# Routing without two-SBUF-input vector steps, one whole-row load of A, shared transpose banks, and first loads planned with the rest, in a fused linear-attention and mixture-of-adapters kernel

## The chip, the cores and the metric

The kernel runs on one core of one Trainium2 chip. The metric is the device time of one execution in microseconds (us), as the median over several executions. One profiled execution of each kernel gives a trace; its span is about 1.8 us shorter than the time of the same execution (span 137.4 us for 139.16 us in the kernel before), so spans and times are not mixed below.

Five engines matter. PE is the matrix engine (PEld is its weight load), DVE the vector engine, ACT the scalar engine, POOL the GpSimd engine, and SP only issues DMA transfers. Each works through its own list of instructions in order: in the trace of the kernel before, ACT stands 16.97 us at one step whose input has not come, and does none of its later steps meanwhile. SBUF is the on-chip memory that the loads fill. PSUM is the memory that PE writes its results to, here in banks that the steps take and give back.

On this one core a run is called slow when it is more than 1.5% above the fastest run of the same kernel in its call. Slow does not mean a lower clock here: in the first call the slow runs of the kernel before had granted PE clocks of 0.942 to 0.971, the fast ones 0.936 to 0.973.

## The reference

Linear attention with cosine and sine weights of the position, then a top-2 mixture of rank-16 adapters on its result. Sizes: 8 batches, 8 heads, 576 positions, 64 per head, so x has 4608 rows of 512.

```python
# attention, per batch and head
r = np.maximum(x, 0.0)
phi(x) = np.concatenate([r * cos_w, r * sin_w], axis=-1)        # 64 -> 128
kv  = einsum('bhsf,bhsd->bhfd', phi(k), v);   z = sum_s phi(k)
num = einsum('bhsf,bhfd->bhsd', phi(q), kv);  den = phi(q) . z + 1e-06
x   = (num / den), heads side by side: 4608 x 512
# adapters
logits = x @ w_gate                     # 8 experts
w, e   = softmax over the two largest logits
out    = x + sum over those two of w * ((x @ A[e]) @ B[e])      # A: 512x16, B: 16x512
```

## The kernel before

The program is a list of named steps, each with an engine, a modelled cost, a priority, the steps it depends on and the buffers it takes and gives back. A planner written in Python simulates them when the kernel is built and emits them in its simulated order. On the chip that order is fixed: if the model is wrong about when something is ready, the engine simply waits there.

```python
def plan(ops, bufs, slack=0.12):
    ...        # per engine: earliest possible start s of each candidate
        for e, c in by_eng.items():
            s0 = min(c)[0]
            pick = min((x for x in c if x[0] <= s0 + slack), key=lambda x: (x[1], x[0]))
            if best is None or pick[0] < best[0]:
                best = pick
    ...
```

The steps of one batch: SP loads k, q and v (1.18 MB each); ACT makes kp = phi(k), in 9 pieces of two instructions; POOL casts v to bf16 (vb); PE accumulates kvz from kp and vb, and ACT copies it to kvs. The steps of one group g of 128 rows (36 groups; two half-groups of 64 rows each): POOL scales q (qp), PE transposes it (qTp), DVE copies it out with the relu (qT), PE multiplies with kvs (nd), DVE normalises (rden, then xt), PE transposes (xTp), DVE copies (xT), PE makes logits and x·A together (za). Every third group the routing follows for three groups at once: DVE (m8, lm, u, ge), ACT (sigmoid sg), DVE (wg, zg), PE and DVE (zTp, zT), then PE makes dx, ACT copies it (osb) and SP stores it. Each pair of batches has nine groups: four of the first batch, four of the second, and a last one shared by both. So both q buffers of a pair come free only when POOL has done the qp of the shared group. There are three buffers each for k, q and v.

The parts that the change touches:

```python
    # loads of batch 0 first, written out ahead of the plan; then A, in four
    # scattered loads (runs of 16 floats, 64 bytes)
    for name in "kqv":
        for a in range(2):
            load(name, 0, a, 2)
    ...
    for ci in range(DCH):
        nc.sync.dma_start(out=AWf[:, ci, 0:ER],
                          in_=moe_A[:, ci * 128:(ci + 1) * 128, :].transpose([1, 0, 2]))
    ...
    # routing
    nc.vector.tensor_tensor(out=lm, in0=m8[:, :, 0], in1=m8[:, :, 1], op=ALU.add)
    ...
    ge = p_sm.tile([NP, TRI, E], FP32, name="ge")              # in SBUF
    nc.vector.tensor_tensor(out=ge, in0=lg, in1=m8[:, :, 1:2].to_broadcast(...), op=ALU.is_ge)
    ...
    nc.vector.tensor_tensor(out=wg, in0=ge, in1=sg, op=ALU.mult)
    ...
    # the plan: loads of batch 0 depend on "start" and emit nothing;
    # loads of later batches depend on their buffer alone
    op("start", "none", 0.0, 0, none, lat=2.2)
    op("weights", "none", 0.0, 0, none, lat=15.0)
    ...
    # the qp of one half-group; the shared group gives both q buffers back
    op(("qp", g, y), "POOL", 0.91, p - 14 + 4 * y, ...,
       give=["qf"] if b in done else [])
```

PSUM banks: `big` 2 (kvz, nd), one for qTp, one shared by xTp and zTp, one for za, one for dx.

Of the kernel before, what the change touches and what calls it, by code (L numbers as in the profile page):

```python
# [12 lines left out]
ALU = mybir.AluOpType  # L13
# [12 lines left out]

def plan(ops, bufs, slack=0.12):

# [6 lines left out]
    for n, o in ops.items():  # L35
# [3 lines left out]
        if not o.deps:  # L39
            cand.append(n)  # L40
    order = []
    while waiting:
        best = None
        by_eng = {}
        for n in cand:
            o = ops[n]
            if any(not free[p] for p in o.take):
                continue
            s = max([eng_free.get(o.eng, 0.0)]
                    + [ops[d].end + (ops[d].lat if ops[d].eng != o.eng else 0.0) for d in o.deps]  # L50
                    + [min(free[p]) for p in o.take])
            by_eng.setdefault(o.eng, []).append((s, o.prio, n))
        for e, c in by_eng.items():
            s0 = min(c)[0]
            pick = min((x for x in c if x[0] <= s0 + slack), key=lambda x: (x[1], x[0]))
            if best is None or pick[0] < best[0]:
                best = pick
        if best is None:
            raise RuntimeError(f"no step can go: {sorted(waiting)[:20]}")
        s, _, n = best  # L60
        o = ops[n]
        o.start, o.end = s, s + o.cost
        eng_free[o.eng] = o.end
        for p in o.take:
            free[p].remove(min(free[p]))
        for p in o.give:
            free[p].append(o.end + o.lat)
        cand.remove(n)
        del waiting[n]
        for m in succ.get(n, ()):  # L70
            nblock[m] -= 1
            if nblock[m] == 0:
                cand.append(m)
        order.append(n)
# [4 lines left out]
def kernel(  # L79
# [43 lines left out]
    ps_big = ctx.enter_context(tc.tile_pool(name="ps_big", bufs=2, space=PS))  # L123
    ps_qt = ctx.enter_context(tc.tile_pool(name="ps_qt", bufs=1, space=PS))
    ps_tp = ctx.enter_context(tc.tile_pool(name="ps_tp", bufs=1, space=PS))
    ps_za = ctx.enter_context(tc.tile_pool(name="ps_za", bufs=1, space=PS))
# [5 lines left out]
    def load(name, b, a, parts):  # L132
        src = {"q": q, "k": k, "v": v}[name]
        if a == 0:
# [5 lines left out]
            in_=dv[:, a * n:(a + 1) * n])  # L140

    for name in "kqv":
        for a in range(2):
            load(name, 0, a, 2)

# [25 lines left out]

    AWf = persist.tile([NP, DCH, ER + E], FP32, name="AWf")
    for ci in range(DCH):
        nc.sync.dma_start(  # L174
            out=AWf[:, ci, 0:ER],
            in_=moe_A[:, ci * 128:(ci + 1) * 128, :].transpose([1, 0, 2]),
        )
    nc.sync.dma_start(
        out=AWf[:, :, ER:ER + E],
        in_=moe_w_gate.rearrange("(c p) e -> p c e", p=128),  # L180
    )
    Bf = persist.tile([NP, DM], FP32, name="Bf")
    nc.sync.dma_start(out=Bf, in_=moe_B.rearrange("e r d -> (e r) d"))
    AW = persist.tile([NP, DCH, ER + E], BF16, name="AW")
    Ball = persist.tile([NP, DM], BF16, name="Ball")

    def weights_cast(i):
        nc.vector.tensor_copy(*((AW, AWf), (Ball, Bf))[i])

# [53 lines left out]
    st = [dict() for _ in range(G)]  # L243
    tri_za, tri_zgT = {}, {}

# [9 lines left out]
    def q_t(g):  # L255
        qps = st[g].pop("qp")
        qTp = ps_qt.tile([NP, HP, 2, 2, SP], BF16, name="qTp")
        for y, qp in enumerate(qps):
# [40 lines left out]
    def x_t(g):  # L299
        xt = st[g]["xt"]  # L300
        xTp = ps_tp.tile([NP, DCH, NP], BF16, name="xTp", tag="tp")
        for c in range(DCH):
# [10 lines left out]
    def za_mm(g):  # L313
        t, i = divmod(g, TRI)
        xT = st[g].pop("xT")
        if i == 0:
            tri_za[t] = ps_za.tile([NP, TRI, ER + E], FP32, name="za")
        za = tri_za[t]
# [6 lines left out]
    def route_a(t):  # L325
# [3 lines left out]
        for i in range(TRI):  # L329
            nc.vector.max(out=m8[:, i, :], in_=za[:, i, ER:ER + E])  # L330

        lm = p_sm.tile([NP, TRI], FP32, name="lm")
        nc.vector.tensor_tensor(out=lm, in0=m8[:, :, 0], in1=m8[:, :, 1], op=ALU.add)  # L333
        u = p_sm.tile([NP, TRI, E], FP32, name="u")
        nc.vector.scalar_tensor_tensor(out=u, in0=lg, scalar=2.0,
                                       in1=lm.to_broadcast([NP, TRI, E]),
                                       op0=ALU.mult, op1=ALU.subtract)
        ge = p_sm.tile([NP, TRI, E], FP32, name="ge")
        nc.vector.tensor_tensor(out=ge, in0=lg,
# [23 lines left out]
    def z_t(t):  # L363
        zg = tri_zgT[t]
        zTp = ps_tp.tile([NP, TRI, NP], BF16, name="zTp", tag="tp")
        for i in range(TRI):
# [24 lines left out]
    def store(g):  # L391
        osb = st[g].pop("osb")
        for y, (b, x) in enumerate(groups[g]):
# [5 lines left out]
          "kvs": 4, "xt": 8, "xT": 3, "zT": 3, "osb": 12,  # L399
          "big": 2, "qTp": 1, "tp": 1, "za": 1, "dx": 1}  # L400
    ops = {}

    def op(name, *args, **kw):
        ops[name] = Op(*args, **kw)
# [5 lines left out]
    LEAD = 2  # L410
    op("start", "none", 0.0, 0, none, lat=2.2)
    op("weights", "none", 0.0, 0, none, lat=15.0)
    for i in range(2):
        op(("w", i), "DVE", 0.35, 10 + 10 * i, lambda i=i: weights_cast(i), deps=["weights"])
    for b in range(B):
        for n, name in enumerate("kqv"):
            due = 10 * GB * (b - LEAD) + 4 * n
            parts = 2 if b == 0 else 1
            for a in range(parts):
                if b == 0:  # L420
                    op(("ld", name, b, a), "SP", 0.65, due, none, deps=["start"],
                       take=[name + "f"] if a == 0 else [], lat=1.3)
                else:
                    op(("ld", name, b, a), "SP", 0.65, due,
                       lambda name=name, b=b: load(name, b, 0, 1),
                       take=[name + "f"], lat=1.3)
                op((name, b, a), "DMA", 3.02 / parts, due, none,
                   deps=[("ld", name, b, a)], lat=0.4)
# [22 lines left out]
    for g in range(G):  # L451
# [4 lines left out]
        for y in range(2):  # L456
# [5 lines left out]
        op(("qt", g), "PE", 0.45, p - 4, lambda g=g: q_t(g),  # L462
           deps=[("qp", g, 0), ("qp", g, 1)], take=["qTp"], give=["qp"] * 2)
        op(("qr", g), "DVE", 0.6, p - 2, lambda g=g: q_relu(g),
           deps=[("qt", g)], take=["qT"], give=["qTp"])
        op(("nd", g), "PE", 0.35 if len(bs) == 1 else 0.5, p + 2, lambda g=g: attn(g),
# [4 lines left out]
        op(("xT", g), "PE", 0.23, p + 10, lambda g=g: x_t(g),  # L471
           deps=[("xt", g)], take=["tp"])
        op(("xo", g), "DVE", 0.34, p + 12, lambda g=g: x_out(g),
           deps=[("xT", g)], take=["xT"], give=["tp"])
        op(("za", g), "PE", 0.26, p + 16, lambda g=g: za_mm(g),
           deps=[("xo", g), ("w", 0)], take=["za"] if i == 0 else [], give=["xT"])
        if i == TRI - 1:
# [5 lines left out]
            op(("zt", t), "PE", 0.17, p + 21, lambda t=t: z_t(t),  # L483
               deps=[("rb", t)], take=["tp"])
            op(("zo", t), "DVE", 0.3, p + 22, lambda t=t: z_out(t),
               deps=[("zt", t)], take=["zT"], give=["tp"])
        p = 10 * (3 * t + 2) + 24 + 6 * i
        op(("dx", g), "PE", 0.45, p, lambda g=g: dx_mm(g),
           deps=[("zo", t), ("w", 1)], take=["dx"],
           give=["xt"] + (["zT"] if i == TRI - 1 else []))  # L490
# [37 lines left out]
```

## Time and profile before

| | before |
|---|---|
| median time | 140.7 us (139.75 to 141.67, 3 runs) |
| span of the profiled run, granted PE clock | 137.4 us, 0.960 |
| first rden on DVE (the first normalised group) | 31.8 us |
| first to last rden | 92.3 us, of which DVE is busy 84.5 |
| after the last rden's start | 13.4 us |

The page of the kernel before: busy time of each engine; then digits, one for each of 40 slices of the span (3.4 us each), the busy tenths of the slice (row DMA: the core's DMA engines); the DMA rate in the same slices; and the engines' shares of the chain of work that ended last.

```profile
PE 90.7 (66%) x1580; PEld 66.9 (49%) x1580; DVE 95.1 (69%) x268; ACT 81.8 (60%) x193; POOL 84.4 (61%) x170
...
DVE  0263230027999999889869898999989899995500
...
POOL 4009960499599795999980899999599900000000
...
DMA  4999899999999999999999999598932727162765
GB/s 134 366 376 202 160 376 402 393 392 389 391 393 380 394 397 405 389 394 401 373 394 398 395 392 339 149 211 207 372 107 57 177 57 172 24 159 51 182 159 118
...
DVE 47%; PE 23%; SPq 10%; ACT 9%; DMA 5%; issue 3%; ACTq 0%
```

No engine is busy more than 69% of the span, but DVE is at eight or nine tenths (once six) from the eleventh slice until the tail: it bounds the middle. Before that DVE does little, but for the third and the tenth slice, and the DMA rate dips to 202 and 160 GB/s in two of them.

The timeline of the kernel before, lines of SP, ACT, DVE and POOL. The columns are start, duration, engine, source line, operation, output and input, number of instructions, and in brackets the idle time just before and what ended it. For a line of SP (SPq) the duration is the time in which it issued, waits between its issues included.

```profile
3.81 9.45 SPq L174 DMA_DIRECT2D AWf<-in_moe_A_dram  x4
...
14.52 0.43 SPq L138 DMA_DIRECT2D kf<-in_k_dram  x1
...
20.92 0.51 ACT L204 ACTIVATE kp<-kf,cos_tab 128x256 bf16<-128x256 f32 x1 [16.97 <-DMA kf<-in_k_dram]
...
30.50 0.57 ACT L231 CAST kvs<-kvz 128x520 bf16<-128x520 f32 x1
...
31.76 0.21 DVE L290 RECIPROCAL rden<-nd 128x8 f32<-128x8 f32 x1 [1.57 <-PE nd L277]
...
62.18 2.42 DVE L333 TENSOR_TENSOR lm<-m_1306 128x3 f32<-128x3 f32 x1
...
62.18 2.23 POOL L212 CAST vb_130<-vf 128x1152 bf16<-128x1152 f32 x2
...
76.13 0.48 POOL L250 TENSOR_SCALAR qp<-qf,cos_tab 128x256 bf16<-128x256 f32 x1 [4.42 <-DMA qf<-in_q_dram]
```

Three things are to be seen. The four scattered loads of A hold SP for 9.45 us, so k of batch 1 is issued only at 14.52. The planner had placed kp of batch 1 ahead of kp of batch 0 in ACT's list, so ACT waits 16.97 us for that k, and kvs of batch 0, which the first group needs, comes at 30.50. And a DVE step on three columns, lm, took 2.42 us beside two POOL casts.

Durations of the same step over its 12 and 36 executions, from the tile view of the kernel before: minimum, median and maximum in ns, then the first and the last start in us.

```profile
L353 DVE TENSOR_TENSOR wg<-ge,sg x12: 173/294/634, 39.9 to 128.3; 128x24 f32<-128x24 f32 x12
...
L290 DVE RECIPROCAL rden<-nd x36: 197/207/209, 31.8 to 124.0; 128x8 f32<-128x8 f32 x36
```

The stretch from first to last rden, from the windows view of the kernel before: the stretch and its length, busy us (instructions) of PE, PEld, DVE, ACT and POOL, then granted PE clock, DMA share and GB/s.

```profile
31.76:124.03 92.27, 79.34 (x1448) 59.98 (x1446) 84.53 (x236) 64.08 (x155) 67.86 (x133) 0.96 0.86 292
```

### The profile page before, as it was taken

How to read it: one execution, taken by the hardware profiler on the slowest of the kernel's cores; microseconds unless marked ns; L12 is line 12 of the kernel's file. 1: busy time of each engine (PE TensorE's matmuls, PEld its weight loads, DVE VectorE, ACT ScalarE, POOL GpSimd, SP SyncE). 2: the span in 40 equal slices, each digit the busy share in tenths (PEclk: the TensorE clock that was granted, in tenths of full speed). 3: DMA queues.
4: the chain of work that ended last, by engine and by line, in shares of the span. 5: the costliest groups of instructions: out<-in, count | busy, mean ns of one | idle time of the engine just before them, and what ended most of it. 6: DMA issues, size and time to landing. Idle time of an engine off the chain costs nothing.

```text
span 137.4 us, 4094 instructions
## 1 busy us (share of the span) xinstructions
PE 90.7 (66%) x1580; PEld 66.9 (49%) x1580; DVE 95.1 (69%) x268; ACT 81.8 (60%) x193; POOL 84.4 (61%) x170
## 2 busy tenths in 40 slices
PE   0004200459886998993699999878998996967430
PEld 0003100358674865772587668555766865644100
DVE  0263230027999999889869898999989899995500
ACT  7100009999078999985538986993899142321440
POOL 4009960499599795999980899999599900000000
PEclk9999999999999999999559999999999999999995
DMA  4999899999999999999999999598932727162765
GB/s 134 366 376 202 160 376 402 393 392 389 391 393 380 394 397 405 389 394 401 373 394 398 395 392 339 149 211 207 372 107 57 177 57 172 24 159 51 182 159 118
DMA packets 23331, 38.55 MB, mean 281 GB/s; under 512 B 6288, under 2 KB 6288, under 8 KB 23312
## 3 DMA queue, kind: packets, MB, share of 16 engines
q1 hardware_dynamic: 23312, 38.30, 83.9%
q8 instruction: 12, 0.20, 0.6%
q14 instruction: 7, 0.06, 0.1%
HBM read 28.85 MB, written 9.44 MB: 279 GB/s over the span
## 4 chain that ended last, share of the span: by engine, by line
DVE 47%; PE 23%; SPq 10%; ACT 9%; DMA 5%; issue 3%; ACTq 0%
DVE xt L292 15%; SPq L174 7%; ACT kp L204 7%; DVE qT L266 7%; DVE xT L310 6%; DMA kf<-in_k_dram 5%; DVE zg L355 5%; DVE rden L290 4%; PE dx L382 4%; PE kvz L224 4%; DVE lm L333 3%; PE nd L277 3%; PE za L320 3%; PE xTp L303 3%; PE qTp L260 2%
## 5 line engine op out<-in xcount | busy, mean ns | idle before, releaser
L250 POOL TENSOR_SCALAR qp<-qf,cos_tab 128x256 bf16<-128x256 f32 x72 | 34.8, 483 | 20.0 <-DMA qf<-in_q_dram 20.0
L204 ACT ACTIVATE kp<-kf,cos_tab 128x256 bf16<-128x256 f32 x66 | 33.1, 502 | 17.0 <-DMA kf<-in_k_dram 17.0
L250 POOL TENSOR_SCALAR qp<-qf,sin_tab 128x256 bf16<-128x256 f32 x72 | 35.0, 487 | 0.0
L266 DVE TENSOR_SCALAR qT<-qTp 128x1024 bf16<-128x1024 bf16 x36 | 24.6, 682 | 14.7 <-PE qTp L260 14.6
L388 ACT COPY osb<-dx 128x512 f32<-128x512 f32 x36 | 20.9, 580 | 23.0 <-PE dx L382 22.8
L260 PE MATMUL qTp<-ident,qp 128*128 128x128 bf16 x288 | 24.6, 233 | 12.6 <-POOL qp L250 11.8
L204 ACT ACTIVATE kp<-kf,sin_tab 128x256 bf16<-128x256 f32 x66 | 32.8, 497 | 0.0
L292 DVE TENSOR_TENSOR xt<-nd,rden 128x512 bf16<-128x512 f32 x36 | 24.9, 691 | 1.2
L260 PEld LDWEIGHTS <-qp 128*128 128x128 bf16 x288 | 18.9, 104 | 13.9 <-POOL qp L250 12.9
L224 PEld LDWEIGHTS <-kp 64*128 64x128 bf16 x576 | 11.2, 99 | 14.6 <-ACT kp L204 11.6
L303 PE MATMUL xTp<-ident,xt 128*128 128x128 bf16 x144 | 14.8, 228 | 5.2 <-DVE xt L292 5.1
L310 DVE COPY xT<-xTp 128x512 bf16<-128x512 bf16 x36 | 15.1, 419 | 3.4 <-PE xTp L303 2.5
L277 PE MATMUL nd<-kvs,qT 128*128 128x65 bf16 x256 | 14.5, 202 | 3.6 <-DVE qT L266 1.9
L381 PE MATMUL dx<-xt,ident 128*128 128x512 bf16 x36 | 13.9, 386 | 3.9 <-ACT osb L388 3.5
L320 PE MATMUL za<-AW,xT 128*128 128x136 bf16 x144 | 15.0, 229 | 2.1 <-DVE zg L355 1.3
L382 PE MATMUL dx<-Ball,zT 128*128 128x512 bf16 x36 | 14.0, 388 | 2.2 <-DVE zT L373 1.8
L277 PEld LDWEIGHTS <-qT 128*128 128x128 bf16 x256 | 11.4, 104 | 7.3 <-DVE qT L266 4.1
L303 PEld LDWEIGHTS <-xt 128*128 128x128 bf16 x144 | 10.1, 101 | 9.9 <-DVE xt L292 6.6
L320 PEld LDWEIGHTS <-xT 128*128 128x128 bf16 x144 | 10.7, 101 | 5.3 <-issue 1.6
L224 PE MATMUL kvz<-vb_128,kp 64*128 64x65 bf16 x216 | 5.9, 208 | 11.0 <-ACT kp L204 11.0
L290 DVE RECIPROCAL rden<-nd 128x8 f32<-128x8 f32 x36 | 7.3, 204 | 4.2 <-PE nd L277 3.3
L231 ACT CAST kvs<-kvz 128x520 bf16<-128x520 f32 x8 | 4.7, 592 | 8.8 <-PE kvz L224 8.7
(73 smaller groups left out, 84.1 us busy)
## 6 DMA issues: line engine op xcount, KB each, us to landing
out_dram<-osb SPq DMA_DIRECT2D x72, 128.0 KB, 3.0
kf<-in_k_dram SPq DMA_DIRECT2D x7, 1152.0 KB, 10.3
qf<-in_q_dram SPq DMA_DIRECT2D x7, 1152.0 KB, 7.9
vf<-in_v_dram SPq DMA_DIRECT2D x7, 1152.0 KB, 13.1
kf<-in_k_dram SPq DMA_DIRECT2D x2, 576.0 KB, 4.1
qf<-in_q_dram SPq DMA_DIRECT2D x2, 576.0 KB, 7.2
vf<-in_v_dram SPq DMA_DIRECT2D x2, 576.0 KB, 9.2
AWf<-in_moe_A_dram SPq DMA_DIRECT2D x4, 64.0 KB, 7.3
```

What stands on the lines that cost most here:

```text
L204: nc.scalar.activation(kp[:, :, i, :], tin["k", b][:, :, x, :], AF.Relu, bias=0.0, scale=tab[:, x:x + 1])
L224: nc.tensor.matmul(out=kvz_t[b][:, e, i * W:(i + 1) * W], lhsT=kps[b, x][ps, i], rhs=vb[ps, i, x, :], start=(x == 0), stop=(x == X - 1))
L250: nc.gpsimd.tensor_scalar(out=qp[:, :, i, :], in0=tin["q", b][:, :, x, :], scalar1=tab[:, x:x + 1], scalar2=1.0, op0=ALU.mult, op1=ALU.mult)
L260: nc.tensor.transpose(out=qTp[:, i, :, y, :], in_=qp[:, i], identity=ident)
L266: nc.vector.tensor_scalar_max(qT, qTp.rearrange("f i e y p -> f (i e) (y p)"), 0.0)
L277: nc.tensor.matmul(out=nd[:, gg, cs], lhsT=qT[:, h, :], rhs=kv_sb[b0][:, h, :], start=True, stop=True)
L292: nc.vector.tensor_tensor(out=xt, in0=nd_v[:, :, :, 0:D], in1=rden.rearrange("p (g j) -> p g j", g=2).to_broadcast([NP, 2, 4, D]), op=ALU. ...
L303: nc.tensor.transpose(out=xTp[:, c, :], in_=xt[:, c * 128:(c + 1) * 128], identity=ident)
L310: nc.vector.tensor_copy(xT, xTp)
L320: nc.tensor.matmul(out=za[:, i, :], lhsT=xT[:, c, :], rhs=AW[:, c, :], start=(c == 0), stop=(c == DCH - 1))
L382: nc.tensor.matmul(out=dx, lhsT=zT[:, i, :], rhs=Ball, start=False, stop=True)
L388: nc.scalar.copy(osb, dx)
```

## The change

Its intent: take away the routing steps of DVE that read two SBUF operands, because they contend with POOL; take A's scattered loads out of SP's way by loading whole 2 KB rows and turning them with 16 PE transposes; let the three kinds of transposes share two rotating banks; and let the planner know that batch 0's loads come first, so that its model of the start is true.

```diff
-def plan(ops, bufs, slack=0.12):
+def plan(ops, bufs, slack=0.05):
@@ banks
-    ps_qt = ctx.enter_context(tc.tile_pool(name="ps_qt", bufs=1, space=PS))
-    ps_tp = ctx.enter_context(tc.tile_pool(name="ps_tp", bufs=1, space=PS))
+    ps_t = ctx.enter_context(tc.tile_pool(name="ps_t", bufs=2, space=PS))
@@ A, in whole rows
+    def load_a():
+        nc.sync.dma_start(out=Af, in_=moe_A.rearrange("e (g l) r -> (e g) l r", l=FL))
+    def a_cast():
+        nc.vector.tensor_copy(Ab, Af)
+    def a_turn():
+        wt["T"] = ps_big.tile([FL, R, NP], BF16, name="aT", tag="big")
+        for r in range(R):
+            nc.tensor.transpose(out=wt["T"][:, r, :], in_=Ab[:, :, r], identity=ident)
+    def a_out(j):                      # four copies into AW: DVE, ACT, DVE, ACT
+        ...
@@ routing
+            za_t[t] = ps_za.tile([NP, ZC + TRI * E], FP32, name="za")
+            tri_za[t] = za_t[t][:, 0:ZC].rearrange("p (t w) -> p t w", t=TRI)
...
-        nc.vector.tensor_tensor(out=lm, in0=m8[:, :, 0], in1=m8[:, :, 1], op=ALU.add)
+        nc.vector.tensor_reduce(out=lm, in_=m8[:, :, 0:2], axis=AXL.X, op=ALU.add)
...
-        ge = p_sm.tile([NP, TRI, E], FP32, name="ge")
+        ge = za_t[t][:, ZC:ZC + TRI * E].rearrange("p (t e) -> p t e", e=E)   # in PSUM
@@ the plan
-    op("start", "none", 0.0, 0, none, lat=2.2)
-    op("weights", "none", 0.0, 0, none, lat=15.0)
+    op("start", "SP", 0.8, -1e9, none)
+    op("ld_a", "SP", 0.5, due0 + 2, load_a, lat=1.3)
...
-                if b == 0:
-                    op(("ld", name, b, a), "SP", 0.65, due, none, deps=["start"], ...)
-                else:
-                    op(("ld", name, b, a), "SP", 0.65, due,
-                       lambda name=name, b=b: load(name, b, 0, 1), take=[name + "f"], lat=1.3)
+                op(("ld", name, b, a), "SP", 0.5, due + a,
+                   lambda name=name, b=b, a=a, parts=parts: load(name, b, a, parts),
+                   take=[name + "f"] if a == 0 else [], lat=1.3)
```

More of the change, by code (lines that the diff above doesn't have):

```diff
@@ L41, in plan @@
     order = []
+    rank = {n: i for i, n in enumerate(ops)}
     while waiting:
@@ L51, in plan @@
                     + [min(free[p]) for p in o.take])
-            by_eng.setdefault(o.eng, []).append((s, o.prio, n))
+            by_eng.setdefault(o.eng, []).append((s, o.prio, rank[n], n))
         for e, c in by_eng.items():
@@ L59, in plan @@
             raise RuntimeError(f"no step can go: {sorted(waiting)[:20]}")
-        s, _, n = best
+        s, _, _, n = best
         o = ops[n]
@@ L140, in load @@
             in_=dv[:, a * n:(a + 1) * n])
-    for name in "kqv":
-        for a in range(2):
-            load(name, 0, a, 2)
     pos_i = persist.tile([NP, X], mybir.dt.int32, name="pos_i")
@@ L170, with load_gb, gb_cast @@
     make_identity(nc, ident)
-    AWf = persist.tile([NP, DCH, ER + E], FP32, name="AWf")
-    for ci in range(DCH):
-        nc.sync.dma_start(
-            out=AWf[:, ci, 0:ER],
-            in_=moe_A[:, ci * 128:(ci + 1) * 128, :].transpose([1, 0, 2]),
-        )
-    nc.sync.dma_start(
-        out=AWf[:, :, ER:ER + E],
-        in_=moe_w_gate.rearrange("(c p) e -> p c e", p=128),
-    )
+    FL = 32
+    Af = persist.tile([NP, FL, R], FP32, name="Af")
+    Ab = persist.tile([NP, FL, R], BF16, name="Ab")
+    Gf = persist.tile([NP, DCH, E], FP32, name="Gf")
     Bf = persist.tile([NP, DM], FP32, name="Bf")
-    nc.sync.dma_start(out=Bf, in_=moe_B.rearrange("e r d -> (e r) d"))
     AW = persist.tile([NP, DCH, ER + E], BF16, name="AW")
     Ball = persist.tile([NP, DM], BF16, name="Ball")
-    def weights_cast(i):
-        nc.vector.tensor_copy(*((AW, AWf), (Ball, Bf))[i])
+    wt = {}
+    def load_a():
+        nc.sync.dma_start(out=Af, in_=moe_A.rearrange("e (g l) r -> (e g) l r", l=FL))
+    def load_gb():
+        nc.sync.dma_start(out=Gf, in_=moe_w_gate.rearrange("(c p) e -> p c e", p=128))
+        nc.sync.dma_start(out=Bf, in_=moe_B.rearrange("e r d -> (e r) d"))
+    def a_cast():
[5 more added lines that the diff above has]
+    def a_out(j):
+        src = wt["T"].rearrange("k r (e c j) -> k j c e r", e=E, j=4)[:, j]
+        dst = AW[FL * j:FL * j + FL, :, 0:ER].rearrange("k c (e r) -> k c e r", e=E)
+        if j % 2:
+            nc.scalar.copy(dst, src)
+        else:
+            nc.vector.tensor_copy(dst, src)
+    def gb_cast():
+        nc.vector.tensor_copy(AW[:, :, ER:ER + E], Gf)
+        nc.vector.tensor_copy(Ball, Bf)
     kps, kv_sb = {}, {}
@@ L243 @@
     st = [dict() for _ in range(G)]
-    tri_za, tri_zgT = {}, {}
+    tri_za, tri_zgT, za_t = {}, {}, {}
+    ZC = TRI * (ER + E)
     def q_phi(g, y):
@@ L256, in q_t @@
         qps = st[g].pop("qp")
-        qTp = ps_qt.tile([NP, HP, 2, 2, SP], BF16, name="qTp")
+        qTp = ps_t.tile([NP, HP, 2, 2, SP], BF16, name="qTp", tag="t")
         for y, qp in enumerate(qps):
@@ L300, in x_t @@
         xt = st[g]["xt"]
-        xTp = ps_tp.tile([NP, DCH, NP], BF16, name="xTp", tag="tp")
+        xTp = ps_t.tile([NP, DCH, NP], BF16, name="xTp", tag="t")
         for c in range(DCH):
@@ L316, in za_mm @@
         if i == 0:
-            tri_za[t] = ps_za.tile([NP, TRI, ER + E], FP32, name="za")
+            za_t[t] = ps_za.tile([NP, ZC + TRI * E], FP32, name="za")
+            tri_za[t] = za_t[t][:, 0:ZC].rearrange("p (t w) -> p t w", t=TRI)
         za = tri_za[t]
@@ L364, in z_t @@
         zg = tri_zgT[t]
-        zTp = ps_tp.tile([NP, TRI, NP], BF16, name="zTp", tag="tp")
+        zTp = ps_t.tile([NP, TRI, NP], BF16, name="zTp", tag="t")
         for i in range(TRI):
@@ L399 @@
           "kvs": 4, "xt": 8, "xT": 3, "zT": 3, "osb": 12,
-          "big": 2, "qTp": 1, "tp": 1, "za": 1, "dx": 1}
+          "big": 2, "t": 2, "za": 1, "dx": 1}
     ops = {}
@@ L410 @@
     LEAD = 2
-    op("start", "none", 0.0, 0, none, lat=2.2)
-    op("weights", "none", 0.0, 0, none, lat=15.0)
-    for i in range(2):
-        op(("w", i), "DVE", 0.35, 10 + 10 * i, lambda i=i: weights_cast(i), deps=["weights"])
+    op("start", "SP", 0.8, -1e9, none)
+    due0 = -10 * GB * LEAD
+    op("ld_a", "SP", 0.5, due0 + 2, load_a, lat=1.3)
+    op("a", "DMA", 0.7, due0 + 2, none, deps=["ld_a"], lat=0.4)
+    op("ld_gb", "SP", 1.0, due0 + 12, load_gb, lat=1.3)
+    op("gb", "DMA", 1.5, due0 + 12, none, deps=["ld_gb"], lat=0.4)
+    op("a_cast", "DVE", 0.35, -10, a_cast, deps=["a"])
+    op("a_turn", "PE", 1.2, -10, a_turn, deps=["a_cast"], take=["big"])
+    for j in range(4):
+        op(("a_out", j), "ACT" if j % 2 else "DVE", 0.65, -9, lambda j=j: a_out(j),
+           deps=["a_turn"] + ([("a_out", i) for i in range(3)] if j == 3 else []),
+           give=["big"] if j == 3 else [])
+    op("gb_cast", "DVE", 0.5, 5, gb_cast, deps=["gb"])
     for b in range(B):
@@ L419 @@
             for a in range(parts):
-                if b == 0:
-                    op(("ld", name, b, a), "SP", 0.65, due, none, deps=["start"],
-                       take=[name + "f"] if a == 0 else [], lat=1.3)
-                else:
-                    op(("ld", name, b, a), "SP", 0.65, due,
-                       lambda name=name, b=b: load(name, b, 0, 1),
-                       take=[name + "f"], lat=1.3)
-                op((name, b, a), "DMA", 3.02 / parts, due, none,
+                op(("ld", name, b, a), "SP", 0.5, due + a,
+                   lambda name=name, b=b, a=a, parts=parts: load(name, b, a, parts),
+                   take=[name + "f"] if a == 0 else [], lat=1.3)
+                op((name, b, a), "DMA", 3.02 / parts, due + a, none,
                    deps=[("ld", name, b, a)], lat=0.4)
@@ L462 @@
         op(("qt", g), "PE", 0.45, p - 4, lambda g=g: q_t(g),
-           deps=[("qp", g, 0), ("qp", g, 1)], take=["qTp"], give=["qp"] * 2)
+           deps=[("qp", g, 0), ("qp", g, 1)], take=["t"], give=["qp"] * 2)
         op(("qr", g), "DVE", 0.6, p - 2, lambda g=g: q_relu(g),
-           deps=[("qt", g)], take=["qT"], give=["qTp"])
+           deps=[("qt", g)], take=["qT"], give=["t"])
         op(("nd", g), "PE", 0.35 if len(bs) == 1 else 0.5, p + 2, lambda g=g: attn(g),
@@ L471 @@
         op(("xT", g), "PE", 0.23, p + 10, lambda g=g: x_t(g),
-           deps=[("xt", g)], take=["tp"])
+           deps=[("xt", g)], take=["t"])
         op(("xo", g), "DVE", 0.34, p + 12, lambda g=g: x_out(g),
-           deps=[("xT", g)], take=["xT"], give=["tp"])
+           deps=[("xT", g)], take=["xT"], give=["t"])
         op(("za", g), "PE", 0.26, p + 16, lambda g=g: za_mm(g),
-           deps=[("xo", g), ("w", 0)], take=["za"] if i == 0 else [], give=["xT"])
+           deps=[("xo", g), ("a_out", 3), "gb_cast"], take=["za"] if i == 0 else [], give=["xT"])
         if i == TRI - 1:
@@ L483 @@
             op(("zt", t), "PE", 0.17, p + 21, lambda t=t: z_t(t),
-               deps=[("rb", t)], take=["tp"])
+               deps=[("rb", t)], take=["t"])
             op(("zo", t), "DVE", 0.3, p + 22, lambda t=t: z_out(t),
-               deps=[("zt", t)], take=["zT"], give=["tp"])
+               deps=[("zt", t)], take=["zT"], give=["t"])
         p = 10 * (3 * t + 2) + 24 + 6 * i
         op(("dx", g), "PE", 0.45, p, lambda g=g: dx_mm(g),
-           deps=[("zo", t), ("w", 1)], take=["dx"],
+           deps=[("zo", t), "gb_cast"], take=["dx"],
            give=["xt"] + (["zT"] if i == TRI - 1 else []))
```

## The prediction

> **What bounds the kernel now.** The span is 137.4 us (runs: median 140.7).
>
> 1. Start. The timeline shows DVE's first rden at 31.8 us. It needs kvs of batch 0, which ACT writes at 30.5, because ACT's program has four kp steps of batch 1 before those of batch 0. They wait 17.0 us for kf of batch 1 (groups view), issued only at 14.5 us: four scattered loads of A hold the SP queue from 3.8 to 13.3 us (timeline), and the DMA rate falls to 202 and 160 GB/s in the fourth and fifth of 40 slices, against about 390.
> 2. Steady, 31 to 128 us: DVE is busy 85 to 94% (windows view) and holds 47% of the chain of waits. Three groups take about 8.0 us (88.46 to 96.42).
> 3. Tail, 127.2 to 137.4 us: a serial chain.
>
> **What the change does.**
>
> - Start: A comes in one load of 2 KB rows, issued third; kf of batch 1 should be issued near 6 us and land near 15. In the new instruction order ACT has kp of batch 0 first, then two copies of A, then kvs of batch 0. Then v bounds: 4.0 MB of first loads at 390 GB/s land near 12.5 us; the v casts end near 15.3, kvz (2 us in the trace) near 17.4, kvs near 18, first rden near 19, sooner by 12 to 13 us, all on the critical path.
> - Added: DVE's cast of A (0.45 us), 16 transposes on PE (estimate 2 us from the cold qTp), two copies each on DVE and ACT (estimate 0.65 each), while v is awaited. Critical: 0 to 1 us.
> - Routing: the Trainium skill, "SBUF — State Buffer", section Who interferes with whom, says that a DVE instruction with two SBUF inputs contends with a GpSimd instruction that reads SBUF. The trace agrees: lm mostly takes 0.164 us, but 2.42 beside two POOL casts of v (62.18) and 0.48 twice; wg takes 0.173 at best, 0.316 in the mean. The excess, 2.9 + 1.7 = 4.6 us, goes, with ge in PSUM and a reduction of one input. DVE bounds there; I take 3.5 us.
> - Shared PSUM banks: qTp may run one ahead, but DVE seldom waits for PE in the steady stretch: 0 to 1 us. The smaller slack reorders steps: about 0.
>
> **Can the rest follow?** 38 MB at 390 GB/s is 97 us: DMA could end near 100. POOL (84 us busy) begins at 10 us and paces 2.3 us a group against DVE's 2.55; its lead shrinks by up to 7 us, as batch 1's q lands only about 6 us sooner. ACT has 82 us, PE 91 us of work in about 120. I give back 1 to 2 us.
>
> **Sum.** 140.7 - 12.5 - 3.5 + 1.3 = 126.0 us, range 121.5 to 131. Faster by over 2%: 0.96; within 2%: 0.03; slower: 0.01.
>
> **What the profile would show.** First rden near 19 us; no dip of the DMA rate between 10 and 17 us; SP without a stall at A; every lm and wg between 0.15 and 0.22 us; DVE busy near 91 us in a span near 123; POOL ending near 97 us; three groups in 7.6 us.
>
> **What would make it wrong.** Loads meet stores sooner, so q or k of a middle batch is late and DVE waits; POOL's lead runs out; PE, packed denser, keeps the granted clock of 0.5, seen in two slices of before, for longer; the two rotating PSUM banks put qTp behind a waiting xTp or zTp; or A's copies, serial across DVE and ACT, delay v's cast and kvs.

## The result, and the profile after

The changed kernel took a median of 132.03 us (131.04 to 132.35, 4 runs, all fast), beside 140.22 us for the kernel before (now 4 runs). The ratio is 0.9388, with a 95% interval of 0.9295 to 0.9481. Ratios here are the mean time of one kernel's fast runs over that of the other's in the same rounds, so not quite the ratio of the medians. The gain is 6% where the prediction had 10%; 132.0 lies above its range of 121.5 to 131.

The page of the kernel after, the same rows, and that of the granted PE clock (slices of 3.3 us). The trace's records of the clock begin at 20.6 us; the nines before that rest on no record.

```profile
PE 93.0 (71%) x1596; PEld 69.1 (53%) x1596; DVE 91.5 (70%) x271; ACT 83.3 (64%) x195; POOL 83.9 (64%) x170
...
DVE  0192959943999989999699413998699987984200
...
POOL 4008999899796999999600999999999600000000
PEclk9999999967999999999999995999999999976855
DMA  4999999999999999999999999977826654433663
GB/s 124 378 393 374 398 391 390 394 390 387 391 391 386 395 393 402 392 396 406 354 405 399 404 388 389 375 259 191 208 65 149 149 136 113 106 69 80 161 158 84
...
DVE 33%; PE 26%; POOL 13%; DMA 12%; issue 7%; ACT 4%; SPq 1%; POOLq 0%; ACTq 0%; DVEq 0%
```

The dip of the DMA rate at the start is gone: it stays near 390 GB/s from the second slice to about 85 us, with the DMA engines busy nine tenths or more. DVE starts early. But its row now has two holes that the kernel before did not have: slices 9 and 10 (4, 3) and slices 23 to 25 (4, 1, 3). POOL has two empty slices just before the second hole. The chain, which held 47% DVE before, now holds 13% POOL and 12% DMA.

The tile view and the windows view of the kernel after:

```profile
L354 DVE TENSOR_REDUCE lm<-m_1305 x1: 159/159/159, 51.1 to 51.1; 128x3 f32<-128x6 f32 x1
L374 DVE TENSOR_TENSOR wg<-za,sg x12: 172/173/182, 26.4 to 120.6; 128x24 f32<-128x24 f32 x12
...
L309 DVE RECIPROCAL rden<-nd x36: 197/198/208, 18.9 to 116.1; 128x8 f32<-128x8 f32 x36
```

```profile
18.90:116.07 97.17, 78.27 (x1448) 59.88 (x1446) 79.44 (x239) 71.29 (x172) 73.91 (x144) 0.96 0.90 314
```

The eleven other lm took 159 or 160 ns. These views give the ledger of the two profiled spans, in us:

| | before | after | difference |
|---|---|---|---|
| start, to the first rden | 31.8 | 18.9 | −12.9 |
| first to last rden | 92.3 | 97.2 | +4.9 |
| of that, DVE busy | 84.5 | 79.4 | −5.1 |
| of that, DVE idle | 7.7 | 17.7 | +10.0 |
| from the last rden to the end | 13.4 | 14.5 | +1.1 |
| span | 137.4 | 130.6 | −6.8 |

Both gains that the change aimed at came, −12.9 and −5.1. Ten microseconds went into new idle time of DVE. The tail's 1.1 us fell in slices with a granted clock of 0.5 to 0.8 (last digits of the clock row); why the clock was lower there was not tested.

Where the idle time is, read from the timeline of the kernel after, lines of all engines in order of time:

```profile
1.72 0.47 SPq L182 DMA_DIRECT2D Af<-in_moe_A_dram  x1
...
5.86 2.03 SPq L138 DMA_DIRECT2D kf<-in_k_dram  x1
...
17.33 0.60 ACT L249 CAST kvs<-kvz 128x520 bf16<-128x520 f32 x1 [3.14 <-PE kvz L242]
...
27.22 0.38 PE L388 MATMUL zTp<-ident,zg 128*128 128x128 bf16 x3 [1.74 <-DVE zg L376]
...
27.98 2.16 PE L242 MATMUL kvz<-vb_118,kp 64*128 64x65 bf16 x72
...
30.86 0.61 PE L279 MATMUL qTp<-ident,qp 128*128 128x128 bf16 x8
...
31.51 0.69 DVE L285 TENSOR_SCALAR qT<-qTp 128x1024 bf16<-128x1024 bf16 x1 [3.51 <-PE qTp L279]
...
49.56 5.64 SPq L416 DMA_DIRECT2D out_dram<-osb  x6
...
53.46 0.48 POOL L269 TENSOR_SCALAR qp<-qf,sin_tab 128x256 bf16<-128x256 f32 x1
...
56.33 0.37 SPq L138 DMA_DIRECT2D kf<-in_k_dram  x1
59.32 0.37 SPq L138 DMA_DIRECT2D vf<-in_v_dram  x1
59.79 3.17 SPq L416 DMA_DIRECT2D out_dram<-osb  x4
63.05 1.28 SPq L138 DMA_DIRECT2D qf<-in_q_dram  x2
...
72.11 0.48 POOL L269 TENSOR_SCALAR qp<-qf,cos_tab 128x256 bf16<-128x256 f32 x1 [7.83 <-DMA qf<-in_q_dram]
...
74.44 0.69 DVE L285 TENSOR_SCALAR qT<-qTp 128x1024 bf16<-128x1024 bf16 x1 [1.72 <-PE qTp L279]
...
75.71 2.23 POOL L230 CAST vb_120<-vf 128x1152 bf16<-128x1152 f32 x2
...
76.91 0.75 PE L242 MATMUL kvz<-vb_120,kp 64*128 64x65 bf16 x36 [1.61 <-POOL vb_120 L230]
...
79.07 0.66 PE L341 MATMUL za<-AW,xT 128*128 128x136 bf16 x4
...
79.77 0.32 DVE L351 MAX8 m_2035<-za 128x8 f32<-128x8 f32 x3 [4.30 <-PE za L341]
```

The large hole reads backwards like this. DVE waits until 79.77 for za. PE has that za behind parts of kvz of batch 5 in its list, and kvz waits for the cast of v (POOL, 75.71 to 77.94). The cast stands behind four qp halves of batch 5 in POOL's list, and POOL could not start those before 72.11, because q of batch 5 had not landed: 7.83 us of idle time. That q was issued at 63.05. Its buffer had been free since about 54, when POOL ended the shared group of batches 2 and 3 (the line at 53.46). Between the two, SP worked through what stood in front in its list: the end of six stores, then k and v of batch 6 and four stores, whose data were not more urgent. Much of that time SP waited: in the built program each transfer waits for the completion of the eighth transfer before it, and k and v of batch 6 went out at 56.33 and 59.32, just after such completions (56.27 and 59.26 in the trace). Once issued, q needed 9 us to land in a stream that was already full.

Why did this not hurt before? The line of POOL at 76.13 us, shown of the kernel before, is the same step: the first use of q of batch 5 there too (88 qp instructions, 22 groups, precede it). It came 4.0 us later than in the kernel after. But at that moment DVE before had begun only 17 normalisations, so five groups of work lay between POOL and DVE, and POOL's wait of 4.42 us ended without a hole in DVE's row. In the kernel after DVE stood at 22 when this q arrived: it had caught up with POOL entirely. The new start and the new routing had moved DVE's 22nd normalisation 15.7 us forward (71.8 instead of 87.5) and this load only 4. This paragraph is a reading of two traces.

The small hole, at 28 to 31.5 us, is of PE's making: the qTp that DVE waits for stands behind a zTp that waits 1.74 us for zg, behind za, and behind 2.16 us of kvz of batch 1.

### The profile page after: what moved, and what is told of

The parts are those of the page before. It is cut to its first block, busy times and chain, and to the rows that moved or that the text cites. A ratio compares the mean times of both kernels' runs of the same rounds, so it can differ in the third digit from the quotient of the medians.

```text
span 130.6 us, 4137 instructions
## 1 busy us (share of the span) xinstructions
PE 93.0 (71%) x1596; PEld 69.1 (53%) x1596; DVE 91.5 (70%) x271; ACT 83.3 (64%) x195; POOL 83.9 (64%) x170
## 2 busy tenths in 40 slices
DMA packets 19315, 38.55 MB, mean 295 GB/s; under 512 B 2144, under 2 KB 2144, under 8 KB 19296
## 4 chain that ended last, share of the span: by engine, by line
DVE 33%; PE 26%; POOL 13%; DMA 12%; issue 7%; ACT 4%; SPq 1%; POOLq 0%; ACTq 0%; DVEq 0%
DMA qf<-in_q_dram 12%; DVE xt L311 11%; POOL qp L269 9%; DVE qT L285 8%; PE kvz L242 7%; DVE xT L329 4%; PE dx L402 4%; PE za L341 4%; PE qTp L279 4%; PE dx L403 3%; ACT osb L409 3%; DVE zg L376 3%; PE xTp L322 2%; DVE rden L309 2%; POOL vb_118 L230 2%
## 5 line engine op out<-in xcount | busy, mean ns | idle before, releaser
L402 PE MATMUL dx<-xt,ident 128*128 128x512 bf16 x36 | 14.8, 412 | 4.6 <-ACT osb L409 3.8
L403 PE MATMUL dx<-Ball,zT 128*128 128x512 bf16 x36 | 15.1, 419 | 0.2 <-DVE zT L394 0.2
L242 PEld LDWEIGHTS <-kp 64*128 64x128 bf16 x576 | 12.0, 104 | 5.5 <-issue 4.8
L296 PE MATMUL nd<-kvs,qT 128*128 128x65 bf16 x256 | 13.6, 198 | 1.1 <-DVE xt L311 0.7
L341 PEld LDWEIGHTS <-xT 128*128 128x128 bf16 x144 | 10.1, 101 | 7.1 <-DVE xT L329 4.2
L194 PE MATMUL aT<-ident,Ab 128*32 128x128 bf16 x16 | 1.9, 315 | 9.6 <-DVE Ab L189 9.6
L388 PE MATMUL zTp<-ident,zg 128*128 128x128 bf16 x36 | 4.1, 221 | 5.5 <-DVE zg L376 3.0
L403 PEld LDWEIGHTS <-zT 128*128 128x128 bf16 x36 | 3.6, 99 | 7.5 <-issue 5.4
## 6 DMA issues: line engine op xcount, KB each, us to landing
vf<-in_v_dram SPq DMA_DIRECT2D x7, 1152.0 KB, 14.2
```

The lines of the kernel that those rows point to most:

```text
L242: nc.tensor.matmul(out=kvz_t[b][:, e, i * W:(i + 1) * W], lhsT=kps[b, x][ps, i], rhs=vb[ps, i, x, :], start=(x == 0), stop=(x == X - 1))
L296: nc.tensor.matmul(out=nd[:, gg, cs], lhsT=qT[:, h, :], rhs=kv_sb[b0][:, h, :], start=True, stop=True)
L341: nc.tensor.matmul(out=za[:, i, :], lhsT=xT[:, c, :], rhs=AW[:, c, :], start=(c == 0), stop=(c == DCH - 1))
L403: nc.tensor.matmul(out=dx, lhsT=zT[:, i, :], rhs=Ball, start=False, stop=True)
```

## The experiments

Theory A: what is missing is the order in SP's queue (q of batch 5 behind later needs), and the rest is order on PE; neither is a lack of bandwidth or of engine time. Rival B: DMA runs at 390 GB/s without a pause to 85 us, so loads cannot come sooner, and moving one only makes another late. Rival C: the shared transpose banks, or the smaller slack, made the new holes. For the gains there are the separate questions of what the routing, the load of A and the new plan of loads are each worth.

Twelve kernels ran, in three calls, each on another chip; each call has its own runs of the kernel before (medians 140.24, 140.77 and 141.16 us). Between calls, compare the ratios. All results were correct.

### Move q of batch 5 forward in SP's queue

Only the order of issues on SP changes: k and v of batch 6 and the stores of two groups go behind q of batch 5.

```diff
-    for n in plan(ops, NB):
+    seq = plan(ops, NB)
+    late = [("ld", "k", 6, 0), ("ld", "v", 6, 0), ("st", 6), ("out", 6), ("st", 7), ("out", 7)]
+    ...   # move these to just behind ("ld", "q", 5, 0)
+    for n in seq:
         ops[n].fn()
```

> The changed kernel, with one edit to the order of the SP queue alone: the load of q for batch 5 goes in front of the loads of k and v for batch 6 and of four stores, as early as its buffer is free. Theory A (a late load behind the head of the SP queue): in the changed kernel q of batch 5 was issued at 63.05 us though POOL had freed its buffer near 54, it landed at 72, and POOL waited 7.8 us. Here it is issued near 55 and lands near 64; POOL's wait falls under 2 us, DVE's idle time between 72 and 80 us (about 6 us) goes, and the time is 126.5 to 129 us. Theory B (the DMA rate of 390 GB/s is used up from 3 to 86 us, so any order has something late): the wait moves to v or k, the gain is under 1.5 us, 130.5 or more.

Measured: 125.31 us median (124.7 to 126.17, 4 fast runs), ratio 0.8971 (0.8856 to 0.9087). From the timeline, the waits and the windows of this kernel:

```profile
56.18 0.51 SPq L138 DMA_DIRECT2D qf<-in_q_dram  x1
```

```profile
POOL qp L269 <- DMA qf<-in_q_dram: 10.5, 2, 8.7
```

```profile
19.60:111.60 92.00, 75.40 (x1436) 59.51 (x1447) 79.52 (x239) 71.06 (x172) 73.84 (x144) 0.96 0.95 330
```

The columns of a wait are us in total, times, and the longest. Here q was issued 6.9 us sooner; of the two waits of POOL the longest, 8.7, is the one at the start, the other is for q of batch 3, and none for q of batch 5 is left. DVE's busy time in the stretch is what it was (79.5), and the stretch is 92.0 instead of 97.2. The mean rate there is 330 GB/s instead of 314 only because about the same bytes moved in less time: the last load of the kernel landed at 85.9 us instead of 86.9. The full stream ran no faster, so what counted was which load came first. One reordering of issues gives about 6 us (6.7 by medians), more than the expectation had, and B falls: k and v of batch 6, now later, were not missed. Of the 6.5 us between the two profiled spans 5.2 lie in the stretch and 2.0 in the tail after the last rden (12.5 instead of 14.5 us), less 0.7 at the start; why the tail is shorter was not tested.

### Own banks, and the old slack

```diff
@@ own_banks
-    ps_t = ... bufs=2
+    ps_qt = ... bufs=1      # qTp
+    ps_tp = ... bufs=1      # xTp, zTp
@@ slack_as_before
-def plan(ops, bufs, slack=0.05):
+def plan(ops, bufs, slack=0.12):
```

> The changed kernel with one PSUM bank for qTp and one for xTp and zTp as before (the planner orders some steps anew). Prediction's theory: worth 0 to 1 us, time 132 to 133. Rival: the rotating banks put qTp behind a waiting xTp or zTp and cost part of the missing 6 us; then the time falls to 131 or less.

> The changed kernel with the planner's slack back at 0.12. Prediction's theory: worth about 0, 131 to 133 us. If the order of steps is as sensitive as q5_sooner shows, it moves the time by 2 us or more either way, with POOL's longest wait for q going with it.

Measured: own banks 132.8 us (132.45 to 132.97, 4 fast runs), ratio 0.9513 (0.9456 to 0.957). The mean is 132.76, beside 131.86 for the kernel after: 0.9 us for the shared banks by the means, 1.7 by the ratios. It has the late q too: POOL waits 7.33 us for q of batch 5.

```profile
71.70 0.48 POOL L270 TENSOR_SCALAR qp<-qf,cos_tab 128x256 bf16<-128x256 f32 x1 [7.33 <-DMA qf<-in_q_dram]
```

Its small hole is there too, with a wait of 2.13 us (the planner also reorders some steps in this kernel). The old slack gave 132.83 us; its fast runs, 131.93 and 131.65, have a ratio of 0.9352 (0.9271 to 0.9433), the same as after. It has the late q too, with a POOL wait of 9.7 us, and the small hole with 3.52 us. Neither is the cause of the holes, so C falls.

### The routing: undone in after, undone in the repaired version, and done alone in before

The edit is the two routing hunks of the diff above, taken back or put in alone.

> The changed kernel with the old routing (mask in SBUF, sum by an operation of two SBUF inputs), the order of all engines as in the changed kernel. If DVE bounds as predicted: some lm and wg of 0.3 to 2.4 us again, 2 to 4.5 us of DVE time back, time 134 to 136 us. If late loads set the pace, the extra DVE time falls into DVE's idle stretches and the time stays within 1 us of 132.

> The kernel of q5_sooner with the old routing. In the changed kernel the old routing cost 6.2 us of DVE time but under 2 us in its one fast run (133.9 against 132.0), as DVE's waits for late loads shrank in exchange. With q of batch 5 in time the theory says that DVE bounds again, so most of the port waits count: 129 to 131.5 us, that is 4 to 6 us over 125.3. If the port waits are absorbed anyway, under 127.5.

> The kernel before with the new routing alone (mask in PSUM, sum by a reduction), everything else and the order of the steps as before. Prediction's theory: every lm and wg at 0.15 to 0.22 us, DVE's busy time down by 4 to 5 us from 95.1, and the time down by 2.5 to 4.6 us, to 136 to 138 us. Rival (other waits take the freed time): under 1.5 us.

Undone in after: 137.01 us median, but one run alone was fast, 133.88; three were slow (136.8 to 138.09, clocks 0.907 to 0.916). DVE busy rose by 6.2 us to 97.7. No ratio comes of one fast run, so this one is inconclusive on time. The fast run, the profiled one, hints at a loss of only 2 us, and its trace shows DVE idle 14.2 us in the stretch instead of 17.7, as if the holes swallowed the rest.

Undone in the repaired version (the one with q of batch 5 moved): 133.58 us, ratio 0.9484 (0.9365 to 0.9602), against 0.8971. The expectation, whose "port waits" are the waits of two-input DVE steps on POOL, had at most 131.5. By fast means that is 132.95 − 125.38 = 7.6 us, with nearly equal times before. By the ratios it is 7.2 us. DVE busy 97.9 instead of 92.0, which is 5.9 us, so part of the 7 us is not explained. Its profiled run was slow, but the lm durations of the tile view are plain:

```profile
L354 DVE TENSOR_TENSOR lm<-m x12: 164/347/1658, 25.5 to 121.4; 128x3 f32<-128x3 f32 x12
```

Done alone in before: 136.95 us, ratio 0.9779 (0.9682 to 0.9876), about 3.1 us; DVE busy fell from 95.1 to 90.2. From the tile view:

```profile
L335 DVE TENSOR_REDUCE lm<-m x12: 159/159/159, 38.4 to 124.8; 128x3 f32<-128x6 f32 x12
```

So the waits of two-input steps on POOL's casts and scalings cost DVE 4.9 us in before, of which 3.1 reached the time. They cost more once q of batch 5 is in time.

### The load of A, and the plan of loads, alone

```diff
@@ a_scattered (in after): the four scattered loads back, no turning on PE
-        nc.sync.dma_start(out=Af, in_=moe_A.rearrange("e (g l) r -> (e g) l r", l=FL))
+        for ci in range(DCH):            # in load_gb, behind batch 0's loads
+            nc.sync.dma_start(out=AWf[:, ci, 0:ER],
+                              in_=moe_A[:, ci * 128:(ci + 1) * 128, :].transpose([1, 0, 2]))
@@ before_loads_ordered (in before): the planner is told that batch 0's loads are first
-                       lambda name=name, b=b: load(name, b, 0, 1),
+                       lambda name=name, b=b: load(name, b, 0, 1), deps=["start"],
```

> The changed kernel with A loaded in four scattered loads as before (after v of batch 0, nothing to turn on PE), the order of the other steps unchanged. If the early start comes from the order on ACT (batch 0 in front of batch 1): first rden stays at 18 to 20 us; but SP is held for about 9 us, so batch 1's loads land 7 to 9 us later, DVE waits after its third group, and the time is 136 to 139 us. If the early start came from A's load instead: first rden goes back to 28 us or later and the time to 139 or more.

> The kernel before with one edit in the planner: the loads of all batches follow the same start, so that it plans batch 0's loads first, as they are issued. A still comes scattered. ACT then has the three kp steps of batch 0 and one of batch 1 in front of kvs of batch 0. Theory: that order alone brings first rden from 31.8 us to 22 to 23 us (kf of batch 1 lands near 21), though SP is still held by A for 9 us; the time falls to 133 to 138 us, less than the 9 us at the start, as the later loads come no sooner. Rival (A's load is what the start hangs on): first rden stays over 28 us, the time within 1.5 us of 140.

With A scattered again: 136.15 us median; fast runs 135.7 and 134.0, a little under the expected 136 to 139, ratio 0.9663 (0.9487 to 0.9839). Against the mean of after, 131.86, that is 3.0 us (3.8 by the ratios). The first rden was at 19.6 us all the same, as expected if the order on ACT, which was the new one here, sets the start. What the scattered loads delay is everything behind them on SP, as the timeline shows:

```profile
3.79 9.83 SPq L184 DMA_DIRECT2D AWf<-in_moe_A_dram  x4
```

With the true plan of first loads alone, in the kernel before: first rden at 22.6 us instead of 31.8, 9 us sooner, but fast runs of 137.87 and 137.63, ratio 0.9826 (0.9728 to 0.9924): only 2.4 us gained. (The median, 139.22, has two slow runs in it.) The profiled run was slow, so its trace is not used for more than the start. This is the result in small: 9 us at the start became 2.4 at the end.

### The hole at 28 us: v sooner, or PE's order

Two ideas for it. Either kvz of batch 1 stands late because v of batch 1 lands late, or it stands in the wrong place in PE's list.

```diff
@@ q5_sooner_v1_sooner, on top of q5_sooner
+    seq.remove(("ld", "v", 1, 0))
+    seq.insert(seq.index(("ld", "q", 1, 0)), ("ld", "v", 1, 0))
@@ q5_sooner_kvz_sooner, on top of q5_sooner: kvz of batch 1 into the time in which PE
@@ waits for zg, and one dx behind the qTp that DVE waits for
+    kv = [("kv", 1, i) for i in range(HP)]
+    seq = [n for n in seq if n not in kv and n != ("dx", 0)]
+    at = seq.index(("zt", 0))
+    seq[at:at] = kv
+    seq.insert(seq.index(("qt", 6)) + 1, ("dx", 0))
```

> The kernel of q5_sooner with one more swap in the SP queue: the load of v for batch 1 goes in front of that of q for batch 1. In the changed kernel and in q5_sooner DVE stands idle for 3.3 to 3.5 us near 28 to 32 us, behind kvz of batch 1, whose v lands at 24.2 us. If v's arrival is what that wait hangs on: v lands about 3 us sooner, the idle stretch falls under 1.5 us, and the time falls by 1 to 2.5 us, to 123 to 124.3. If PE's program order is what it hangs on (kvz of batch 1 and two dx steps in front of qTp), the idle stretch stays at 3 us and the time within 0.7 us of 125.3.

> The kernel of q5_sooner with two moves in PE's program alone: kvz of batch 1 in front of the zT transposes and za of the group before (PE waited 1.7 us there for DVE's zg while kvz's inputs were ready), and the dx step behind the qTp step that DVE waits for. Theory: the idle stretch of DVE near 28 to 32 us (3.3 us) hangs on PE's order; kvz of batch 1 starts near 27 instead of 28.8, the idle stretch halves, and the time falls by 1 to 2.5 us, to 123 to 124.3. Rival: the stretch does not matter, or zT, now later, gives the time back: within 0.7 us of 125.3.

v sooner: 128.08 us, ratio 0.9077 (0.8983 to 0.9171), no gain over 0.8971 and by fast means 2.4 us worse, which neither side of the expectation had. v did land sooner, at 20.15 instead of 23.82 us. But POOL now waited 3.46 us for q of batch 1, which v had been put in front of, and those qp steps stand before the cast of v in POOL's list: the cast began at 27.59 instead of 24.59, kvz came later still, and DVE still waited 3.27 us for that qTp. So the swap is no repair, and it does not test whether an earlier cast of v would help.

kvz sooner: 124.66 us median (122.68 to 126.15); fast runs 124.43, 124.1 and 122.68, ratio 0.8756 (0.8668 to 0.8844). By fast means it is 1.6 us better than moving q alone. Three of its six runs were slow; the means of all runs differ by 0.8 us and the ratios by 3.0, so the size is rough. In its timeline and windows:

```profile
29.29 0.69 DVE L285 TENSOR_SCALAR qT<-qTp 128x1024 bf16<-128x1024 bf16 x1 [0.33 <-PE qTp L279]
```

```profile
19.90:110.00 90.10, 75.67 (x1446) 58.19 (x1443) 79.62 (x239) 71.26 (x173) 73.61 (x143) 0.98 0.97 336
```

The wait of 3.51 us became 0.33, with 0.43 and 0.66 us beside it, and the stretch is 90.1 us. kvz of batch 1 began at 26.42 here, though v landed no sooner (24.04). The order on PE was the cause of the small hole; the two moves were not run apart. This is the best version: 12% below the kernel before.

### Repairs in the planner's terms

The moves above are made by hand. Two versions change only what the planner is told: a fourth q buffer; or loads in the strict order k, q, v by batch, with one half of each shared group's qp done early.

```diff
@@ four_q_buffers
+    p_inq = ctx.enter_context(tc.tile_pool(name="p_inq", bufs=4))     # for q; "qf": 4 in the plan
@@ strict_loads
                 op(("ld", name, b, a), "SP", 0.5, due + a, ...,
-                   take=[name + "f"] if a == 0 else [], lat=1.3)
+                   take=[name + "f"] if a == 0 else [], lat=1.3, deps=prev)
+                prev = [("ld", name, b, a)]
...
-        op(("qp", g, y), "POOL", 0.91, p - 14 + 4 * y, ...
+        op(("qp", g, y), "POOL", 0.91,
+           p - 14 + 4 * y - (45 if len(bs) == 2 and y == 0 else 0), ...
```

> The changed kernel with four input buffers for q instead of three, in the planner too, nothing moved by hand. If the late q load is due to q's buffers (two are freed only with the group that a pair of batches shares), the planner now issues q of batch 5 well in front of k of batch 6 and POOL's 7.8 us wait goes: 125 to 129 us. If it comes from the in-order SP queue whatever the buffers: some other load or store is held, and the time is 130 to 133.

> The changed kernel with the planner made to issue loads strictly as k, q, v of each batch in turn, and to take the shared group's first half of q early so that its buffer is free sooner. Theory: no load for a later batch stands in front of q of batch 5; POOL waits under 3 us in all after the start; 125 to 129 us. Rival (strict order holds the queue behind a buffer that is not free, and DMA stands idle): DMA rate dips under 300 GB/s before 80 us and the time is 130 us or more.

Four buffers: 128.85 us, ratio 0.9101 (0.902 to 0.9182); q of batch 5 was issued at 42.3 us, and POOL still waited 1.5 us for q of batch 6. Why it gains less than moving q by hand was not followed up. Strict order: 125.74 us, ratio 0.8907 (0.8842 to 0.8971), the same as moving q by hand. The waits of that kernel:

```profile
POOL qp L269 <- DMA qf<-in_q_dram: 8.3, 1, 8.3
```

The only wait left for a q is the first one. A rule for the planner does as much as a hand-made move, and it needs no more memory.

## Why the prediction was right or wrong

The direction was right and the size was not: 126.0 us were predicted, with a range of 121.5 to 131.0, and 132.0 were measured.

- **The start, −12.5 predicted, −12.9 in the trace: right.** First rden "near 19", measured 18.90. k of batch 1 was issued at 5.86 ("near 6") and landed at 16.99, two us later than said ("near 15"); kvs was written at 17.33 ("near 18"). There was no dip of the DMA rate and no stall of SP at A.
- **The added turning of A, 0 to 1 us on the critical path: in line.** The 16 transposes took 1.9 us of PE (estimate 2), the copies 0.68 on DVE and 0.57 on ACT (estimate 0.65). No run measured their critical part by itself, but with A scattered, without any turning, first rden came no sooner (19.6 against 18.9).
- **The routing, −3.5 predicted: right in mechanism, and its size was the one term on the safe side.** Every lm took 159 or 160 ns and every wg at most 182 ns. DVE's busy time fell to 91.5 us (near 91 predicted), and by 5.1 us in the stretch. Alone in the kernel before it was worth 3.1 us, and in the version with q of batch 5 moved about 7.
- **Shared banks 0 to 1 us, slack about 0: right.** 0.9 us by the means (1.7 by the ratios), and none for the slack.
- **"Can the rest follow? ... I give back 1 to 2 us": this step failed.** It stands, together with the small terms, for the +1.3 of the sum. It compared totals: 38 MB at 390 GB/s, 84 us of POOL, 91 of PE, all of which fit into 120 us. They do fit: the repaired versions run in 124 to 126 us with the same work. But whether the totals fit does not say when one load arrives. In the stretch DVE's idle time grew by 10.0 us, not by 1.3, and the two holes came from order: q of batch 5 behind less urgent transfers in SP's queue (about 6 us), and the qTp behind kvz on PE (1.6 us by fast means). The prediction did name these risks ("q or k of a middle batch is late and DVE waits; POOL's lead runs out"), and even said that POOL's lead would shrink by up to 7 us, as q of batch 1 would land only about 6 us sooner. That q landed 3.8 us sooner (20.0 instead of 23.8), and the prediction did not follow the lead to later batches: by its 22nd normalisation DVE came 15.7 us sooner, q of batch 5 only 4, and the five groups of lead were gone.
- **POOL "ending near 97", a span "near 123": wrong for the same reason**, about 103 and 130.6. With q of batch 5 moved POOL ended at 96.5 and the span was 124.1. "Three groups in 7.6 us" was met in places: routing began at 37.30, 44.14, 50.78 and 59.46, so 6.8, 6.6 and 8.7 us, with no hole between them.
- **The clock** was named as a risk. It was low in the two slices of the small hole (0.6, 0.7), at the end of the large hole (0.5) and in the tail. In the small hole it added to the damage: kvz of batch 1 took 2.16 us there, and 1.33 us in the version that moves it into PE's gap, where the clock row has a 9. This is a reading of two traces, not an experiment of its own, and kvz of batch 0 took 2.16 us too, at 15.12, where there is no record of the clock. The Trainium skill, "TensorE: Matmul & The Clock Gate", Part 1, says that activity releases the clock and idleness lowers it; the two traces agree with that: in the kernel after, PE is busy four tenths in slices 23 and 24 and the clock is at 0.5 in slice 25, and in the version without the small hole the clock does not drop near 28 us.

With q moved, the sum would have held: 125.3 us against 126.0. That agreement is partly luck, since the routing gave more and the hole at 28 us took some back.

What stays open: the three waits of DVE shown above, 3.51, 1.72 and 4.30 us, make 9.5 us, about what its idle time grew by, but how much of each reached the time is known only roughly, from the two repairs. The rest of about 10 us of idle time in the best version's stretch was not followed up. Nor was it tried to let more than eight transfers be under way.

## What to carry to other kernels

When a change makes the bounding engine start sooner or run faster, list for each stream of loads how much sooner it comes, batch by batch, and compare with the lead that hid it; totals that fit prove nothing about one late load. In-order queues need a check of their own: ask of each urgent load or matmul what stands in front of it, and whether that is needed later. If a planner decides the order, tell it the order of loads, as a dependency, rather than trust its modelled times to a few tenths of a microsecond.

## What the Trainium skill lacked or had wrong

- "SBUF — State Buffer", section Who interferes with whom, says that a DVE instruction with two SBUF inputs contends with a GpSimd instruction that reads SBUF, and the page's summary that the one that comes second blocks until the first ends. The trace agrees in kind, but the page lacks that the block can last over more than one instruction of the winner: lm took 2.42 us, as long as two back-to-back casts on POOL (2.23 us for both). It also gives no cost for a kernel as a whole: here 4.9 us of DVE time for 24 tiny instructions.
- The same page, section Summary: rules for kernel authors, tells one to estimate transfers between HBM and SBUF at about 358 GB/s. Here one core held 374 to 406 GB/s in all slices but one for over 80 us, and an estimate from the page's figure (38.55 MB / 358 GB/s = 108 us) is some 9 us longer than one from the 390 GB/s of the trace (99 us). "HBM Reference", section Specifications (TRN2), is nearer: it says that a core streaming alone measures about 425.
- "DMA: Bandwidth & Descriptors", section Specifications, gives 512 B as the least transfer for full rate. The scattered loads of A, in runs of 64 B, agree: 202 and 160 GB/s in their slices, with the DMA engines busy nine and eight tenths. The page lacks what such loads do to the issuing queue: four loads of 64 KB held SP for 9.45 us and delayed the loads behind them, where one load of the same 256 KB in whole rows held it for 0.47 us.
- The same page, section Latency and other measured facts, gives about 0.6 us to the first byte. It lacks the time from issue to landing in a stream that is already full: here a 1.18 MB load took a median of 11 to 14 us in the kernel after.
- No page covers the order of an in-order issue queue as a bound: a transfer held up for 9 us behind six less urgent ones cost about 6 us of 132, though the totals of every engine and of the loads fitted.
